# Two state-space heads: another start for B's first rows, early products of zeros, another order of the whole work

## The chip, the cores and the metric

The kernel runs on one core of one Trainium2 chip. A core has TensorE (PE; PEld is its loading of weights), VectorE (DVE), ScalarE (ACT), GpSimd (POOL) and SyncE (SP, which here only issues DMAs), an on-chip memory SBUF of 128 partitions, and PSUM, eight banks of 128 x 512 float32 values in which products are summed up. TensorE writes to PSUM alone, and VectorE or ScalarE has to copy the result out (an eviction). The metric is the device time of one execution in microseconds (us); less is better.

## The reference

Two independent heads over a sequence of 2048 steps, 640 channels each; the outputs stand beside each other, 1280 columns in bfloat16.

```
A:  dt = exp(log_dt);  Lam_bar = exp(dt * Lam);  B_bar = ((Lam_bar - 1) / Lam)[:, None] * B     (complex, 640 states)
    h[t] = Lam_bar * h[t-1] + B_bar x[t]
    y[t] = 2 Re(C h[t]) + x[t] * Dskip
B:  k_shift = causal convolution of k with 4 taps per channel
    kv = k_shift * v
    y  = causal convolution of kv with ssm_k (2048 taps per channel, by FFT of length 4096) + kv * ssm_D
    out = q * y
```

## The kernel before

**Head A** cuts the 2048 steps into 128 blocks of 16 and computes the recurrence as a tree. x is loaded transposed by eight transposing DMAs (`ld_x0` to `ld_x7`, L524, two of the 16 positions each). B is loaded in three parts: the first 128 rows as they lie, real and imaginary part (`ld_Braw`, L487), and turned by ten TensorE transposes (`turn_B`, L501) whose result one copy evicts (`ev_B`, L506); the other 512 rows by transposing DMAs (`ld_B1`, `ld_B2`, L491). The upsweep (`up2`, `up1`, `up0`) is products of B with x (L556) and, from `up1` on, of 2x2 rotation blocks RR with the results below (L577). Its first ten steps are called `up21_*` (they need x6 and x7) and `up20_*` (x4 and x5), each 20 products and one eviction (L573). A short recurrence over the blocks (`coarse`, a matter of VectorE with a scan, L656) and the downsweep (`dn`, products L681 and an addition `ad`: on VectorE L699, or on ScalarE as a plain copy L697, in which case TensorE first adds the old value by a product with the identity, L679) follow; then 16 projections by C (`project`, 20 products each, L716, eviction L718, store L722).

**Head B** computes the long convolution as a two-step Fourier transform by matrix products: a first step `s1` (L832, eviction `e1`, L837) with the table F1, a second step `s2` (L850, eviction L863) with the table W, the product of the two spectra (`product`, L874 to L881, on VectorE or POOL), and the way back in `r2` (L895, L900) and `r1` (L916, L928), then stores (L940). This is done in two halves of 320 channels. The convolution with four taps (`conv`, L797 and L798, taps by L197 on VectorE or L198 on ScalarE) comes before, channel block by channel block; its results are written to HBM and read back in another layout (`plane`, `relay`).

**Parameters.** `params` loads Lambda and log_dt by three small DMAs (`ld_par`, L348), turns them by one product (`t_par`, L356), evicts them (L358) and works out rotations from them with many small instructions on VectorE, ScalarE and POOL. `setup` makes the identity I3 and the tables F1, W and IDF with iotas and sines.

**Warm steps.** `warm` multiplies the identity with itself, four products of 512 columns (L516). Nobody reads the result. There are two of them; one stands first in TensorE's list, the other last.

**What sets the order.** All of this is 759 operations with ids in the order in which `build` adds them. The string `ORDER` lists them as id, engine letter (A ScalarE, V VectorE, G POOL, T TensorE, S SyncE) and PSUM bank. `emit` issues them in this order, each engine in its own part of it, and puts in the semaphores that the data need. So the place of an operation in the list decides what it is queued behind, and its letter which engine does it. On SP's queue the order of before begins `ld_B1 ld_x6 ld_x7 ld_B2 ld_B2 ld_B1 ld_x5 ld_x4 ld_k0 ld_sk`; on ScalarE's it begins `ld_Braw ld_par ld_par ld_Braw ld_par dt ev_B`; on TensorE's `warm1 t_par turn_B up21_0 up21_8 up21_4 up21_6`.

Of the kernel before, what the change touches and what calls it, by code (L numbers as in the profile page):

```python
# [9 lines left out]
ALU = mybir.AluOpType  # L10
# [23 lines left out]
class Program:  # L34


    def __init__(self, nc, arena, psum):
        self.nc, self.arena, self.psum = nc, arena, psum
        self.ops, self.groups, self.engine_of = [], [], {}
        self.ncol = arena.shape[1]  # L40

# [177 lines left out]
def setup(c):  # L219
# [47 lines left out]
    for b, off in ((0, 6144.0), (1, 8192.0)):  # L267
# [6 lines left out]
        out=F1.rearrange("p (k s) -> p k s", s=4), in0=bc(s1.rearrange("p (k o) -> p k o", o=1), [128, 64, 4]),  # L274
        in1=bc(me4.rearrange("p (o s) -> p o s", o=1), [128, 64, 4]), op=ALU.mult), outs=[F1], ins=[s1, me4])
# [62 lines left out]
def params(c):  # L338
# [4 lines left out]
    pr = v("YS", 0, 128)  # L343
# [121 lines left out]
class PartA:  # L465
# [14 lines left out]
    def load_B(self, k):  # L480
# [12 lines left out]
        if k == 0:  # L493
            g = P.group(2)
            idn, out = c.I3[:, 0:128], c.v("BT", 0, 1280)

            def mm(e, B):
                Bb = B.bitcast(bf16)
                for r in range(2):
                    for d in range(5):  # L500
                        e.transpose(out=Bb[:, 1024 * r + 128 * d:1024 * r + 128 * d + 128], in_=raw[:, 640 * r + 128 * d:640 * r + 128 * d + 128],  # L501
                                    identity=idn)
            P.add("turn_B", {PPE: .58}, mm, ins=[raw, idn], group=g, nmm=10)

            def ev(e, B):
                c.CP[e](out=out.rearrange("p (r x) -> p r x", r=2), in_=B.bitcast(bf16).rearrange("p (r x) -> p r x", r=2)[:, :, 0:640])  # L506
            P.add("ev_B", {PDVE: .82, PACT: 1.23}, ev, outs=[out], group=g)

    def warm(self, k):

        c, P = self.c, self.c.P
        g = P.group(1)

        def mm(e, B):
            for _ in range(4):
                e.matmul(B[:, 0:512], lhsT=c.I3[:, 0:128], rhs=bc(c.I3[:, 0:1], [128, 512]), start=True, stop=True)  # L516
        P.add(f"warm{k}", {PPE: .864}, mm, ins=[c.I3], group=g, nmm=4)
# [207 lines left out]
class PartB:  # L725
# [91 lines left out]
    def s1(self, what, hf, u):  # L817
# [11 lines left out]
        def mm(e, B):  # L829
            for i in range(8):  # L830
                for b in range(2):
                    e.matmul(B[64 * b:64 * b + 64, 128 * i:128 * i + 128], lhsT=lh[i], rhs=F[:, b, :], start=True, stop=True,  # L832
                             tile_position=(0, 64 * b))
        P.add(f"s1{what}{hf}_{u}", {PPE: .45}, mm, ins=lh + [c.F1], group=g, nmm=16)
# [3 lines left out]
            out=out, in_=B.rearrange("p (n k l s) -> p k s l n", n=8, l=2, s=2)), outs=[out], group=g)  # L838
# [108 lines left out]
def build(c):  # L947

    setup(c)
    params(c)  # L950
    a, b = PartA(c), PartB(c)
    c.a, c.b = a, b
    b.load_small()
    a.warm(0)
    a.warm(1)
# [75 lines left out]
def plain_order(P):  # L1031
# [125 lines left out]
```

## Time and profile before

| | us |
|---|---|
| median of 3 runs | 204.18 (204.13 to 205.32) |
| profiled execution | 205.59 |
| its span, first to last instruction | 203.8 |
| busy: PE / PEld | 181.6 / 121.0 |
| busy: DVE / ACT / POOL | 166.1 / 138.9 / 80.0 |

The busy times are sums over the whole span; TensorE is at 89%, VectorE at 81%, ScalarE at 68%, POOL at 39%. The DMA engines moved 30.12 MB in 107544 packets, nearly all of them under 512 bytes. An engine's share of the span is an average over stages with different limits, so the stretches of 10 us, further down, tell more than this table. In the profile a line number says which line of the program an instruction stems from; "x20" is a count; what stands behind "<-" in square brackets is what ended the wait ahead of the instruction.

### The profile page before, as it was taken

How to read it: one execution, taken by the hardware profiler on the slowest of the kernel's cores; microseconds unless marked ns; L12 is line 12 of the kernel's file. 1: busy time of each engine (PE TensorE's matmuls, PEld its weight loads, DVE VectorE, ACT ScalarE, POOL GpSimd, SP SyncE). 2: the span in 40 equal slices, each digit the busy share in tenths (PEclk: the TensorE clock that was granted, in tenths of full speed). 3: DMA queues.
4: the chain of work that ended last, by engine and by line, in shares of the span. 5: the costliest groups of instructions: out<-in, count | busy, mean ns of one | idle time of the engine just before them, and what ended most of it. 6: DMA issues, size and time to landing. Idle time of an engine off the chain costs nothing.

```text
span 203.8 us, 6975 instructions
## 1 busy us (share of the span) xinstructions
PE 181.6 (89%) x3075; PEld 121.0 (59%) x3079; DVE 166.1 (81%) x225; ACT 138.9 (68%) x167; POOL 80.0 (39%) x64
## 2 busy tenths in 40 slices
PE   3279999999999987767798899999999999999894
PEld 0135444446666744556677666666576877787672
DVE  2194999964999499988999989899999999876931
ACT  2059975476983759999988879989877993291000
POOL 8238970039400900000023294694860506325211
DMA  6999999996998999859969963940524783374785
GB/s 121 176 191 195 133 165 200 127 192 125 182 166 229 309 131 125 181 102 168 118 169 182 119 99 100 197 67 5 120 76 94 155 208 96 107 170 122 166 181 142
DMA packets 107544, 30.12 MB, mean 148 GB/s; under 512 B 102394, under 2 KB 106874, under 8 KB 107514
## 3 DMA queue, kind: packets, MB, share of 16 engines
q1 hardware_dynamic: 107136, 29.34, 80.2%
q10 hardware_dynamic: 378, 0.34, 1.0%
q8 instruction: 24, 0.39, 1.0%
q14 instruction: 6, 0.05, 0.1%
HBM read 10.99 MB, written 7.86 MB: 93 GB/s over the span
## 4 chain that ended last, share of the span: by engine, by line
PE 68%; ACT 16%; DVE 8%; DMA 3%; issue 3%; ACTq 1%; DVEq 0%
PE acc L556 22%; PE acc L716 21%; ACT arena L863 9%; PE acc L850 5%; ACT arena L837 5%; PE acc L895 5%; PE acc L832 4%; PE acc L681 4%; PE acc L577 3%; DMA arena<-in_A_Lambda_re_dram 3%; PE acc L916 2%; DVE arena L928 1%; DVE arena L837 1%; DVE arena L550 1%; DVE arena L718 1%
## 5 line engine op out<-in xcount | busy, mean ns | idle before, releaser
L556 PE MATMUL acc<-arena 128*64 128x512 bf16 x400 | 48.6, 397 | 1.3 <-ACT arena L506 1.3
L716 PE MATMUL acc<-arena 128*128 128x320 bf16 x320 | 46.1, 299 | 1.1 <-issue 0.9
L863 ACT CAST arena<-acc 128x960 bf16<-128x960 f32 (+1 forms) x41 | 36.0, 915 | 7.4 <-PE acc L850 6.4
L716 PEld LDWEIGHTS <-arena 128*128 128x128 bf16 x320 | 30.2, 98 | 14.3 <-issue 1.4
L556 PEld LDWEIGHTS <-arena 128*64 128x64 bf16 x400 | 22.4, 111 | 24.5 <-issue 1.8
L837 ACT CAST arena<-acc 128x1024 bf16<-128x1024 f32 x31 | 30.0, 1035 | 2.8 <-PE acc L832 2.4
L850 PE MATMUL acc<-arena 128*64 128x160 bf16 x512 | 23.2, 236 | 4.4 <-ACT arena L863 3.3
L832 PE MATMUL acc<-arena 128*64 128x128 bf16 x640 | 22.7, 221 | 2.8 <-ACT arena L837 1.4
L850 PEld LDWEIGHTS <-arena 128*64 128x64 bf16 x512 | 17.8, 109 | 11.7 <-ACT arena L863 6.2
L832 PEld LDWEIGHTS <-arena 128*64 128x64 bf16 x640 | 19.1, 110 | 7.7 <-ACT arena L837 2.6
L900 ACT CAST arena<-acc 128x1024 bf16<-128x1024 f32 x16 | 15.7, 1022 | 7.5 <-PE acc L895 7.5
L797 DVE TENSOR_TENSOR arena<-arena 128x2048 bf16<-128x2048 bf16 x15 | 19.9, 1327 | 0.3
L718 DVE TENSOR_TENSOR arena<-acc,arena 128x640 bf16<-128x640 f32 x16 | 13.1, 822 | 8.6 <-PE acc L716 8.3
L877 POOL TENSOR_TENSOR arena<-arena 128x1280 bf16<-128x1280 bf16 x5 | 13.2, 2640 | 16.8 <-DVE arena L874 9.2
L699 DVE TENSOR_TENSOR arena<-acc,arena 128x1024 bf16<-128x1024 f32 x15 | 17.8, 1217 | 1.0 <-PE acc L681 1.0
L881 POOL TENSOR_TENSOR arena<-arena 128x1280 bf16<-128x1280 bf16 x5 | 13.3, 2653 | 8.3 <-DVE arena L877 8.0
L708 POOL TENSOR_TENSOR arena<-arena 128x640 bf16<-128x640 bf16 x7 | 9.7, 1398 | 17.3 <-DMA arena<-in_A_x_dram 17.3
L197 DVE TENSOR_SCALAR arena<-arena 128x2048 bf16<-128x2048 bf16 (+1 forms) x19 | 15.0, 810 | 0.3
L766 POOL TENSOR_TENSOR arena<-arena 128x80 bf16<-128x80 bf16 x2 | 1.8, 878 | 31.8 <-DVE arena L874 31.8
L198 ACT ACTIVATE arena<-arena 128x1024 bf16<-128x1024 bf16 (+3 forms) x14 | 13.8, 1013 | 0.2
L329 POOL TENSOR_TENSOR arena<-arena 128x1024 int32<-128x1024 int32 x4 | 7.5, 1896 | 14.9 <-DVE arena L420 14.9
L681 PE MATMUL acc<-arena 128*128 128x512 bf16 (+2 forms) x50 | 12.1, 328 | 0.4 <-ACT arena L863 0.4
(138 smaller groups left out, 266.7 us busy)
## 6 DMA issues: line engine op xcount, KB each, us to landing
out_dram<-arena SPq DMA_DIRECT2D x32, 160.0 KB, 3.2
arena<-in_B_ssm_k_dram SPq DMA_DIRECT2D x8, 320.0 KB, 6.7
kv_rows<-arena SPq DMA_DIRECT2D x5, 512.0 KB, 3.2
arena<-kv_rows SPq DMA_DIRECT2D x8, 320.0 KB, 6.5
arena<-in_A_x_dram SPq DMA_DIRECT2D x16, 160.0 KB, 2.4
arena<-in_B_q_dram SPq DMA_DIRECT2D x8, 320.0 KB, 5.8
arena<-in_A_B_im_dram ACTq DMA_DIRECT2D x1, 160.0 KB, 2.6
arena<-in_A_B_re_dram ACTq DMA_DIRECT2D x1, 160.0 KB
```

Source lines behind the costliest of these rows:

```text
L197: vm = lambda e: lambda out, in_, by: e.tensor_scalar_mul(out=out, in0=in_, scalar1=by)
L556: e.matmul(o[64 * r:64 * r + 64], lhsT=self.BT[j][:, r, d, :], rhs=self.XP[:, d, 2 * q:2 * q + 2], start=(d == 0), stop=(d == 4), skip_gro ...
L681: e.matmul(B[:, o:o + 128 * k], lhsT=c.RR[:, n, j, :], rhs=A[:, j, q:q + k, 0:128], start=not by_pe, stop=True, skip_group_check=True)
L699: e.tensor_tensor(out=o, in0=b, in1=o, op=ALU.add)
L716: e.matmul(B[:, 512 * b:512 * b + 320], lhsT=lh[j], rhs=self.CT[:, j, 320 * b:320 * b + 320], start=(j == 0), stop=(j == 9))
L718: P.add(f"ev_C{i}", {PDVE: dve(640)}, lambda e, B: e.tensor_tensor(out=ys.rearrange("p (b n) -> p b n", b=2), in0=B.rearrange("p (b n) -> ...
L797: P.add(f"ca{d}_{j}", tt, lambda e: e.tensor_tensor(out=t1, in0=t1, in1=t2, op=ALU.add), outs=[t1], ins=[t1, t2])
L832: e.matmul(B[64 * b:64 * b + 64, 128 * i:128 * i + 128], lhsT=lh[i], rhs=F[:, b, :], start=True, stop=True, tile_position=(0, 64 * b))
L837: P.add(f"e1{what}{hf}_{u}", {PACT: act(1024), PDVE: dve(1024)}, lambda e, B: c.CP[e](out=out, in_=B.rearrange("p (n k l s) -> p k s l n", ...
L850: e.matmul(B[64 * s:64 * s + 64, 512 * b + 160 * i:512 * b + 160 * i + 160], lhsT=c.W[:, k, 64 * b:64 * b + 64], rhs=self.AS[hf][:, k, 160 ...
L863: c.CP[e](out=out, in_=b.rearrange("p r (k j n) -> p r k j n", k=n, j=4) if nj > 1 else b.rearrange("p r (k x) -> p r k x", k=n))
L900: P.add(f"er2{hf}_{u}", {PACT: act(1024), PDVE: dve(1024)}, lambda e, B: c.CP[e](out=out, in_=B.rearrange("p (s n b) -> p b s n", s=2, n=4 ...
```

## The change

It has five parts.

1. **B's first rows.** `turn_B` and `ev_B` become two operations each, one for the real and one for the imaginary half: five transposes into one PSUM bank and one copy of 640 columns. In the new order both raw loads stand first on ScalarE's queue, and the three `ld_par` are on SP's.
2. **Products of zeros.** Six warm steps of two products each in place of two of four; they multiply a block of zeros in YS, which POOL clears (`wz`), and not the identity. The parameters' landing place moves from YS 0 to YS 1280 to make room. All six stand in the first part of TensorE's list, and none at its end.
3. **F1** is stored with its columns in another order (position within 32 innermost), and the first step's eviction reads PSUM accordingly.
4. **Narrow first steps.** An `s1` step whose letter in the order is a lower-case `t` computes its products on half the rows and half the columns; one with `T` computes them as before. The new list holds capital letters only.
5. **A new order**, with other engines for some 80 operations and other PSUM banks. The ids shift, since the warm steps are now added first: an id of before plus seven is the same operation, apart from the warm steps and the turning of B. By name, SP's list now begins `ld_sk ld_par ld_par ld_par ld_x6 ld_x7 ld_B1 ld_B1 ld_x5 ld_x4 ld_k0 ld_B2 ld_B2 ld_x2 ld_x3`; ScalarE's `ld_Braw ld_Braw dt rn rn rn ev_B1 rn ev_B0 ev_up21_0` (`ev_B0` the real half, `ev_B1` the imaginary, `rn` a short exponential); TensorE's `turn_B0 warm2 t_par warm4 warm1 warm5 turn_B1 warm0 warm3 up21_0 up21_4 up21_2 up20_0 up20_2 up20_4 up21_6 up20_8 up20_6`. The coarse recurrence's first product (`cs_v0`) stands ahead of the scaling of C (`gC`) in the new list and behind most of it in the old one. Of the additions of the downsweep `ad2_5`, `ad1_2`, `ad1_0` and `ad0_0` go from VectorE to ScalarE, `ad3_5` and `ad0_9` come back. Eight half products of the spectra go from POOL to VectorE and one the other way; the last two steps of the convolution's fourth channel block (`ca3_0`, `cx3`) go from VectorE to POOL.

```diff
@@ setup
     P.add("f1", {V: .42}, lambda e: e.tensor_tensor(
-        out=F1.rearrange("p (k s) -> p k s", s=4), in0=bc(s1.rearrange("p (k o) -> p k o", o=1), [128, 64, 4]),
-        in1=bc(me4.rearrange("p (o s) -> p o s", o=1), [128, 64, 4]), op=ALU.mult), outs=[F1], ins=[s1, me4])
+        out=F1.rearrange("p (b s k) -> p b s k", b=2, s=4), in0=bc(s1.rearrange("p (b o k) -> p b o k", b=2, o=1), [128, 2, 4, 32]),
+        in1=bc(me4.rearrange("p (o s x) -> p o s x", o=1, x=1), [128, 2, 4, 32]), op=ALU.mult), outs=[F1], ins=[s1, me4])
@@ params
-    pr = v("YS", 0, 128)
+    pr = v("YS", 1280, 128)
@@ load_B
         if k == 0:
-            g = P.group(2)
-            idn, out = c.I3[:, 0:128], c.v("BT", 0, 1280)
-
-            def mm(e, B):
-                Bb = B.bitcast(bf16)
-                for r in range(2):
+            idn = c.I3[:, 0:128]
+            for r in range(2):
+                g, out, part = P.group(1), c.v("BT", 640 * r, 640), raw[:, 640 * r:640 * r + 640]
+
+                def mm(e, B, part=part):
                     for d in range(5):
-                        e.transpose(out=Bb[:, 1024 * r + 128 * d:1024 * r + 128 * d + 128], in_=raw[:, 640 * r + 128 * d:640 * r + 128 * d + 128],
-                                    identity=idn)
-            P.add("turn_B", {PPE: .58}, mm, ins=[raw, idn], group=g, nmm=10)
...
+                        e.transpose(out=B.bitcast(bf16)[:, 128 * d:128 * d + 128], in_=part[:, 128 * d:128 * d + 128], identity=idn)
+                P.add("turn_B", {PPE: .29}, mm, ins=[part, idn], group=g, nmm=5)
+                P.add("ev_B", {PDVE: .5, PACT: .7}, lambda e, B, out=out: c.CP[e](out=out, in_=B.bitcast(bf16)[:, 0:640]), outs=[out], group=g)
@@ warm
+        z = c.v("YS", 0, 130)
+        if k == 0:
+            P.add("wz", {PDVE: .1, PPOOL: .25}, lambda e: e.memset(z, 0.0), outs=[z])
+
         def mm(e, B):
-            for _ in range(4):
-                e.matmul(B[:, 0:512], lhsT=c.I3[:, 0:128], rhs=bc(c.I3[:, 0:1], [128, 512]), start=True, stop=True)
-        P.add(f"warm{k}", {PPE: .864}, mm, ins=[c.I3], group=g, nmm=4)
+            for _ in range(2):
+                e.matmul(B[:, 0:512], lhsT=z[:, 0:128], rhs=bc(z[:, 128:129], [128, 512]), start=True, stop=True)
+        P.add(f"warm{k}", {PPE: .432}, mm, ins=[z], group=g, nmm=2)
@@ s1
-                    e.matmul(B[64 * b:64 * b + 64, 128 * i:128 * i + 128], lhsT=lh[i], rhs=F[:, b, :], start=True, stop=True,
-                             tile_position=(0, 64 * b))
+                    if o.id not in P.narrow:
+                        e.matmul(B[64 * b:64 * b + 64, 128 * i:128 * i + 128], lhsT=lh[i], rhs=F[:, b, :], start=True, stop=True,
+                                 tile_position=(0, 64 * b))
+                        continue
+                    for l in range(2):
+                        ps = slice(64 * l, 64 * l + 64)
+                        e.matmul(B[64 * b:64 * b + 64, 512 * l + 64 * i:512 * l + 64 * i + 64], lhsT=lh[i][ps], rhs=F[ps, b, 64 * l:64 * l + 64],
+                                 start=True, stop=True, tile_position=(64 * l, 64 * b))
...
-            out=out, in_=B.rearrange("p (n k l s) -> p k s l n", n=8, l=2, s=2)), outs=[out], group=g)
+            out=out, in_=(B.rearrange("p (l n s k) -> p k s l n", l=2, n=8, s=2) if o.id in P.narrow
+                          else B.rearrange("p (n l s k) -> p k s l n", n=8, l=2, s=2))), outs=[out], group=g)
@@ build
+    a, b = PartA(c), PartB(c)
+    c.a, c.b = a, b
+    for k in range(6):
+        a.warm(k)
     setup(c)
     params(c)
...
-    a.warm(0)
-    a.warm(1)
@@ ORDER
-    "110G0 85V0 49V0 124A0 51A0 461G0 19G0 116G0 43G0 86V0 128S0 52A0 6G0 7V0 11V0 13V0 20V0 15G0 0G0 1G0 2V0 122T2 3V0 123A0 50A0 "
...
+    "128A0 92V0 38G0 91V0 122S0 56V0 58S0 59S0 129A0 8G0 26G0 127V0 7G0 9V0 117G0 130T2 0G0 3T4 41G0 50G0 13G0 15V0 19V0 34V0 57S0 "
+    "12V0 61T1 62V1 5T4 2T6 95V0 35V0 144S0 94V0 21V0 33V0 126G0 63A0 64V0 32V0 65V0 68A0 71V0 72V0 73V0 66A0 6T5 16V0 74V0 75V0 "
...
@@ the entry
-    order = [(int(x[:-2]), x[-2], int(x[-1])) for x in ORDER.split()] if ORDER else plain_order(c.P)
+    order = [(int(x[:-2]), x[-2].upper(), int(x[-1])) for x in ORDER.split()] if ORDER else plain_order(c.P)
+    c.P.narrow = {int(x[:-2]) for x in ORDER.split() if x[-2] == "t"}
```

More of the change, by code (lines that the diff above doesn't have):

```diff
@@ L40, in __init__ @@
         self.ncol = arena.shape[1]
+        self.narrow = set()
     def group(self, nb):
@@ L831, in mm @@
                 for b in range(2):
-                    e.matmul(B[64 * b:64 * b + 64, 128 * i:128 * i + 128], lhsT=lh[i], rhs=F[:, b, :], start=True, stop=True,
-                             tile_position=(0, 64 * b))
-        P.add(f"s1{what}{hf}_{u}", {PPE: .45}, mm, ins=lh + [c.F1], group=g, nmm=16)
+                    if o.id not in P.narrow:
[6 more added lines that the diff above has]
+                                 start=True, stop=True, tile_position=(64 * l, 64 * b))
+        o = P.add(f"s1{what}{hf}_{u}", {PPE: .45}, mm, ins=lh + [c.F1], group=g, nmm=16)
         gh, n0 = u // 5, 8 * (u % 5)
```

5 lines of the change are left out of this document (removed), and 69 rows, old and new, of the table ORDER.

## The prediction

> **What bounds the kernel now.** I read the chain that ended last first, then the stretches of 10 us, then the instructions of the first 20 us. The chain, at its start and at its end:
>
> ```profile
> 2.79 6.42 DMA arena<-in_A_Lambda_re_dram
> ...
> 9.34 0.18 PE acc L356
> 9.52 1.17 PE acc L501 x10
> ...
> 10.71 1.24 ACT arena L506
> ...
> 11.99 26.62 PE acc L556 x205
> ...
> 200.20 0.84 DVE arena L718
> ...
> 201.31 0.82 PE acc L516 x3
> ```
>
> The first product that counts (L556) starts at 11.99 us. Ahead of it lie a parameter load that took 6.42 us, the parameter product, ten transposes and their copy. From then on the chain is nearly all TensorE. The stretches (start:end, busy time of PE, PEld, DVE, ACT, POOL with counts, clock, DMA share, GB/s) say where that holds:
>
> ```profile
> 0.00:10.00 10.00, 2.55 (x11) 1.12 (x12) 1.52 (x12) 1.50 (x2) 5.75 (x19) 1.00 0.93 146
> 10.00:20.00 10.00, 8.69 (x65) 4.18 (x64) 7.15 (x32) 6.94 (x11) 5.60 (x5) 1.00 1.07 196
> 20.00:30.00 10.00, 10.00 (x90) 4.88 (x88) 9.15 (x7) 9.07 (x13) 8.86 (x10) 1.00 1.15 151
> ...
> 80.00:90.00 10.00, 6.46 (x152) 5.04 (x154) 9.32 (x13) 9.71 (x11) 0.00 (x0) 1.00 0.81 161
> 90.00:100.00 10.00, 7.30 (x194) 6.12 (x188) 9.27 (x11) 9.59 (x12) 0.00 (x0) 1.00 1.13 126
> ```
>
> Three regimes: until 12 us TensorE waits for data; from 12 us the upsweep is TensorE's own work; from 80 to 100 us TensorE is idle for 3.54 + 2.70 us because ScalarE (9.71, 9.59) and VectorE (9.32, 9.27) cannot empty PSUM faster, while POOL does nothing.  So a microsecond saved before 12 us is a microsecond of lead, and the question is whether the middle gives it back.
>
> **The parts of the change.** The profiled execution took 205.59 us, a span of 203.8 and 1.8 around it, 1.4 above the median of 204.18. My terms are differences worked out in its own time; I set them against the median.
>
> *The start.* The early instructions:
>
> ```profile
> 1.16 0.72 ACTq L348 DMA_DIRECT2D arena<-in_A_Lambda_im_dram  x1
> 1.91 0.29 ACTq L348 DMA_DIRECT2D arena<-in_A_log_dt_dram  x1
> 2.24 0.52 ACTq L487 DMA_DIRECT2D arena<-in_A_B_re_dram  x1
> 2.79 0.84 ACTq L348 DMA_DIRECT2D arena<-in_A_Lambda_re_dram  x1
> 3.42 1.89 PE L516 MATMUL acc<-arena 128*128 128x512 bf16 x4 [3.42 <-DVE arena L230]
> 9.56 0.19 DVE L358 COPY arena<-acc 128x30 f32<-128x30 f32 x1 [5.96 <-PE acc L356]
> 12.42 0.18 PEld L556 LDWEIGHTS <-arena 128*64 128x64 bf16 x2 [0.25 <-issue]
> 14.98 1.11 PEld L556 LDWEIGHTS <-arena 128*64 128x64 bf16 x10 [0.25 <-issue]
> 17.93 0.58 SPq L747 DMA_DIRECT2D arena<-in_B_shift_k_dram  x1
> ```
>
> The new order puts both raw loads of B's first rows on ScalarE's queue with nothing before them; the three parameter loads go to SP's queue behind the shift taps and ahead of every transposing load. The first raw load of before landed 2.6 us after its issue:
>
> ```profile
> L487 ACTq DMA_DIRECT2D arena<-in_A_B_im_dram x1: 381/381/381, 0.7 to 0.7; - x1
> ...
> DMA to landing us min/median/max: 2.6/2.6/2.6
> ```
>
> So the real part lands at about 3.4 us and its five transposes (half of 1.17 us) end near 4.0. One warm step of two products at 1.89/4 = 0.47 us each takes TensorE to 4.9. SP issues the taps (0.58) and three parameter loads (0.72 + 0.29 + 0.84 at ScalarE's prices, 0.87 if each took the shortest) by 2.2 to 3.2 us, then 2.6 us to landing: the parameter product at about 5.5, bounds 4.8 and, with the 6.42 us of the chain, 9. Three warm steps (6 x 0.47 = 2.8 us) and five transposes follow: 8.9. ScalarE copies the imaginary half, a short exponential, then the real half. The nearest row for half a copy:
>
> ```profile
> L550 ACT CAST arena<-acc 128x640 bf16<-128x640 f32 x7 | 4.7, 692 | 3.9 <-PE acc L577 2.1 <-PE acc L546 1.7
> ```
>
> Two at 0.69 and the exponential (0.2) end at about 10.5; the last four warm products (1.9 us) end about then, too. With 0.2 for waits the upsweep starts at 10.7 instead of 11.99: **-1.3 us** (bounds -2.5, if the warm products speed up early, and 0, with the late parameters). The twelve zero products replace eight, and as ordered they are ahead of the upsweep, so they cost nothing only as long as the copies end later.
>
> *The pace of the first products.* At 12.42 us weights are loaded in pairs every 0.43 us; from 14.98 on ten take 1.11 us, 0.11 each. In the 2.99 us between 11.99 and 14.98 there are 16 loads, which at the later pace take 1.78: 1.2 us lost to a slow clock (the clock column says 1.00 here, so the pace is the better witness). In before TensorE worked from 3.42 to 5.31, stood still until 9.34 and had 1.35 us of work before the upsweep. In the new order it works from 3.4 with one short wait. I take the whole loss back: **-1.2 us** (bounds -1.2 and 0). The Trainium skill (TensorE: Matmul & The Clock Gate, Part 1) has the full clock follow a busy window of about 3.4 us of a counter that runs on its own, and Part 4 adds that transposes don't count as busy in the same way; by that, a start broken up by transposes and waits may still be cold, which is a rival below.
>
> *What the upsweep then waits for.* Its first step needs the transposing loads x6 and x7, the next two B's second part, the fourth x5 and x4. Two landings of before bracket eight such loads:
>
> ```profile
> L491 SPq DMA_TRANSPOSE arena<-in_A_B_im_dram x1: 1372/1372/1372, 0.7 to 0.7; - x1
> ...
> DMA to landing us min/median/max: 5.5/5.5/5.5
> ...
> L524 SPq DMA_TRANSPOSE arena<-in_A_x_dram x1: 1614/1614/1614, 14.4 to 14.4; - x1
> ...
> DMA to landing us min/median/max: 4.1/4.1/4.1
> ```
>
> First at 6.2, eighth at 18.5: one per 1.76 us, with the DMA share at 0.93 to 1.07. In the new order the first is issued at about 3.0 and lands near 7.5, x7 at 9.3, B's second part at 12.8, x4 at 16.3. Wanted: 10.7, 13.0 (one step of 20 products at 0.113 is 2.26 us) and 17.5. Close, but in time: **+0.2 us** (bounds 0 and 1.0).
>
> *Work moved between engines.* Read by name, the new order moves some 80 instructions. Where the addition of a downsweep step is on ScalarE, TensorE must first add the old value by a product with the identity (L679). Four steps go to ScalarE (six products of 512 columns, four of 256) and two come back (two of 512, five of 128):
>
> ```profile
> 136.17 0.22 PE acc L679
> ...
> 103.15 0.11 PE acc L679
> ...
> L699 DVE TENSOR_TENSOR arena<-acc,arena 128x1024 bf16<-128x1024 f32 x15 | 17.8, 1217 | 1.0 <-PE acc L681 1.0
> L877 POOL TENSOR_TENSOR arena<-arena 128x1280 bf16<-128x1280 bf16 x5 | 13.2, 2640 | 16.8 <-DVE arena L874 9.2 <-PE acc L850 7.6
> L877 DVE TENSOR_TENSOR arena<-arena 128x1280 bf16<-128x1280 bf16 x11 | 9.7, 907 | 0.2
> L797 DVE TENSOR_TENSOR arena<-arena 128x2048 bf16<-128x2048 bf16 x15 | 19.9, 1327 | 0.3
> ```
>
> Six of 0.22 and four of 0.11, less two of 0.22 and five of 0.06 to 0.11, is 0.8 to 1.0 us of TensorE. A third may fall where it idles: **+0.6 us** (bounds 0 and 1.0). VectorE takes over seven spectral half products net, which took POOL 2.64 us each and take it 0.9 (6.3 in all), and gives away two long convolution steps (1.3 each at L797's mean), two of the additions net (1.2 each) and, net, some tap products, scalings and evictions; I take the sum as even, with ScalarE loaded more than before. What counts is the place: between 80 and 100 us POOL, idle now, takes the two convolution steps, 2.6 of VectorE's 18.6 us. If the two full engines shared that relief, TensorE's wait would shrink by 1.3; for ScalarE's added work I take off 0.5: **-0.8 us** (bounds -3 and +3, about half of the 6.2 us idle there either way, since no row shows the middle in another order).
>
> *The rest.* The list of the new order holds no lower-case letter, so the set `narrow` is empty and every first step keeps its wide products. What changes for them is the order of F1's columns and the strides by which the eviction reads PSUM: taken as nothing, bounded by 40 evictions times 28 ns (1035 for L837 against 1007 ns for the plain read of L573):
>
> ```profile
> L837 ACT CAST arena<-acc 128x1024 bf16<-128x1024 f32 x31 | 30.0, 1035 | 2.8 <-PE acc L832 2.4
> L573 ACT CAST arena<-acc 128x1024 bf16<-128x1024 f32 x9 | 9.0, 1007 | 3.8 <-PE acc L556 3.8
> L722 SPq DMA_DIRECT2D out_dram<-arena x1: 332/332/332, 201.1 to 201.1; - x1
> ```
>
> The dead warm step at 201.31 goes, but the last store is issued at 201.1 and lands after 2 to 3 us, so the end stays: 0.
>
> Sum: -1.3 - 1.2 + 0.2 + 0.6 - 0.8 = -2.5; 204.2 - 2.5 = **201.7 us**.
>
> **The rivals.**
>
> *The clock is still slow at 10.7 us.* Against it: over 5 us of products ahead. For it: the four early products of before, 1.89 us, never sped up. The 1.2 us stay: 202.9.
>
> *The lead is given back at 80 us.* There the two evicting engines decide, and ScalarE has more to do than before. Only the relief of POOL's two steps would remain: 204.2 - 0.5 = 203.7.
>
> *POOL holds VectorE* (slower). A long POOL instruction stops VectorE's when that reads two operands from SBUF or runs fast:
>
> ```profile
> 13.39 2.33 POOL L449 TENSOR_TENSOR arena<-arena 128x1280 int32<-128x1280 int32 x1 [6.87 <-DVE arena L378]
> ...
> L268 DVE TENSOR_SCALAR arena<-arena x2: 241/1306/2370, 3.0 to 13.4; 128x32 int32<-128x32 int32 x2
> ```
>
> One of L268's two 32-column instructions took 0.24 us; the other, started with POOL's at 13.4, took 2.37. The Trainium skill (GPSIMD Engine Reference, Specifications) names the same two cases for the shared SBUF interface; the row agrees. The two convolution steps on POOL come to 2.64 x 2048/1280 = 4.2 us each, an estimate from L877. The coarse chain's last step of the second half stands just behind the first of them in VectorE's list; if it is held for 4.2 us while both evicting engines are the bound, and ScalarE's added work eats the rest of the lead (another 0.8 lost instead of won), the time is 201.7 + 0.8 + 4.2 = 206.7. It decides from about 2.5 us of hold.
>
> *The middle does better.* The coarse chain is started ahead of the C scaling, so that downsweep products can fill the 6.2 us of idle TensorE. Half of it filled: 201.7 - 3.1 = 198.6.
>
> **How the numbers follow.** Forecast 201.7 (its own range 200.2 to 203): 0.42. Middle better, 198.6: 0.12. Slow clock, 202.9: 0.10. Lead given back, 203.7: 0.13. POOL holds VectorE, 206.7: 0.23. A measurement of this kernel tells about 1% from no change (202.1 to 206.2). Faster: the better middle and most of the forecast, 0.54; same: the rest of it, slow clock and given back, with a little of the held case, 0.24; slower 0.22. The range: 198.4 to 206.6 leaves out half of the held case and the far tail of the better middle.
>
> **What would show it.** The upsweep's first product at 10 to 11 us with weight loads 0.11 us apart from the start; the parameter product near 5.5; no TensorE wait for DMA between 13 and 25 us; L679 with four to six more columns' worth of products (about 0.9 us); POOL busy in 80 to 100 us and no VectorE instruction of two SBUF operands much above its median there. The prediction is wrong if TensorE's idle time from 80 to 100 us, 6.2 us now, grows by more than the 2.5 us of lead, or if the parameters land at 9 us again.

## The result, and the profile after

| | before | after |
|---|---|---|
| median of 15 runs, us | 205.22 (203.99 to 205.95) | 202.33 (201.56 to 204.01) |
| ratio of the times | | 0.9877 (0.9851 to 0.9903) |
| profiled execution / its span, us | 205.59 / 203.8 | 204.01 / 202.2 |
| busy PE / DVE / ACT / POOL, us | 181.6 / 166.1 / 138.9 / 80.0 | 184.9 / 164.5 / 141.2 / 77.1 |

The change makes the kernel 1.23% faster (0.97 to 1.49%), 2.9 us between the medians; forecast were 2.5 us, 1.2%. The time itself lies 0.6 us above the forecast 201.7, since that was reckoned from before's first three runs (204.18), and its median of 15 is 205.22. The two profiled executions are only 1.6 us apart, because that of after is one of its slowest; why will be seen below. Behind `load_B` the new program's lines are shifted: L573 and L577 are still the upsweep's eviction and rotations, `s1` is L833, its eviction L843, `s2` L857, its eviction L870.

The chain that ended last, of after (start us, length us, what):

```profile
2.49 1.45 SPq L524
...
7.62 4.68 DMA arena<-in_A_B_im_dram
...
23.55 1.28 ACT L369
...
25.07 1.28 ACT L395
...
198.32 0.82 DVE arena L718
```

The head of the chain is now SP's queue with the transposing loads, up to the landing of B's second part (7.62 + 4.68 = 12.30 us); then it is TensorE, broken at 23.5 us by two loads of ScalarE's function tables. The last eviction starts at 198.32 and not at 200.20 us.

The instructions of the first part of after (start us, busy us, engine, line, what, count; in brackets the wait ahead):

```profile
3.27 0.69 PE L501 MATMUL acc<-arena 128*128 128x128 bf16 x5 [3.27 <-DVE arena L242]
4.61 0.23 PE L357 MATMUL acc<-arena 128*128 128x30 bf16 x1
8.64 1.89 POOL L291 TENSOR_TENSOR arena<-arena 128x1024 int32<-128x1024 int32 x1 [0.34 <-DVE arena L247]
8.64 2.07 DVE L269 TENSOR_SCALAR arena<-arena 128x32 int32<-128x32 int32 x2
9.41 1.95 PEld L556 LDWEIGHTS <-arena 128*64 128x64 bf16 x20 [0.68 <-ACT arena L503]
12.44 14.06 PE L556 MATMUL acc<-arena 128*64 128x512 bf16 x120 [0.58 <-DMA arena<-in_A_B_im_dram]
27.59 7.00 PE L556 MATMUL acc<-arena 128*64 128x512 bf16 x60 [1.09 <-ACT arena L573]
34.43 0.60 PE L577 MATMUL acc<-arena 128*64 128x512 bf16 x4
```

The real half of B is turned at 3.27, the parameter product stands at 4.61, the first product that counts at 9.41 us. Its 20 weight loads (1.95 us busy) stand in one unbroken row, and the 20 products take 2.45 us: the pace is the full one. TensorE then waits 0.58 us for B's second part and at 26.5 us 1.09 for ScalarE. The first rotations (L577) start at 34.43 us. In before they start four microseconds later, with 20 products more done by then:

```profile
38.45 0.60 PE L577 MATMUL acc<-arena 128*64 128x512 bf16 x4
```

The stretches of after (start:end, busy time of PE, PEld, DVE, ACT, POOL with counts, clock, DMA share, GB/s):

```profile
0.00:10.00 10.00, 6.71 (x29) 3.05 (x31) 5.93 (x37) 3.29 (x8) 6.44 (x20) 1.00 0.74 143
...
80.00:90.00 10.00, 8.40 (x180) 6.53 (x182) 8.09 (x11) 9.81 (x13) 4.51 (x2) 1.00 0.79 131
90.00:100.00 10.00, 8.77 (x197) 6.82 (x196) 8.79 (x10) 9.62 (x12) 4.84 (x2) 1.00 1.36 157
```

Between 80 and 100 us TensorE is now idle for 1.60 + 1.23 = 2.83 us, 3.4 less than before. That is not a gain of the whole: other stretches that were nearly full now have gaps (TensorE is busy for 9.39 and not 9.91 us between 60 and 70, for 9.54 and not 10.00 between 130 and 140). Over the whole span TensorE's idle time falls from 203.8 - 181.6 = 22.2 to 202.2 - 184.9 = 17.3 us, and the first 10 us alone account for 7.45 - 3.29 = 4.2 of these 4.9. But products that nobody reads count as busy there (5.4 us of them in after, 1.9 in before), so this idle time doesn't measure the gain.

### The profile page after: what moved, and what is told of

It is laid out like the page before. It is cut to its first block, busy times and chain, and to the rows that moved or that the text cites. A ratio compares the mean times of both kernels' runs of the same rounds, so it can differ in the third digit from the quotient of the medians.

```text
span 202.2 us, 6998 instructions
## 1 busy us (share of the span) xinstructions
PE 184.9 (91%) x3086; PEld 123.6 (61%) x3086; DVE 164.5 (81%) x224; ACT 141.2 (70%) x168; POOL 77.1 (38%) x64
## 4 chain that ended last, share of the span: by engine, by line
PE 70%; ACT 15%; DVE 4%; SPq 3%; issue 3%; DMA 2%; DVEq 0%; ACTq 0%
PE acc L716 22%; PE acc L556 20%; ACT arena L870 8%; PE acc L902 6%; PE acc L857 5%; PE acc L833 5%; PE acc L577 4%; ACT arena L843 3%; PE acc L923 3%; PE acc L681 2%; DMA arena<-in_A_B_im_dram 2%; SPq L524 2%; PE acc L546 1%; DVE arena L718 1%; DVE arena L843 1%
## 5 line engine op out<-in xcount | busy, mean ns | idle before, releaser
L870 ACT CAST arena<-acc 128x960 bf16<-128x960 f32 (+1 forms) x41 | 36.3, 918 | 4.7 <-PE acc L857 2.9
L556 PEld LDWEIGHTS <-arena 128*64 128x64 bf16 x400 | 23.6, 108 | 23.5 <-ACT arena L573 2.1
L843 ACT CAST arena<-acc 128x1024 bf16<-128x1024 f32 x29 | 27.9, 1035 | 4.6 <-PE acc L833 4.5
L708 POOL TENSOR_TENSOR arena<-arena 128x640 bf16<-128x640 bf16 x10 | 13.8, 1396 | 38.9 <-DMA arena<-in_A_x_dram 38.9
L857 PE MATMUL acc<-arena 128*64 128x160 bf16 x512 | 23.5, 236 | 4.0 <-ACT arena L870 1.6
L857 PEld LDWEIGHTS <-arena 128*64 128x64 bf16 x512 | 17.9, 109 | 12.1 <-ACT arena L870 4.7
L833 PE MATMUL acc<-arena 128*64 128x128 bf16 x640 | 22.0, 221 | 1.4 <-ACT arena L843 1.0
L907 ACT CAST arena<-acc 128x1024 bf16<-128x1024 f32 x17 | 16.8, 1030 | 8.1 <-PE acc L902 8.0
L833 PEld LDWEIGHTS <-arena 128*64 128x64 bf16 x640 | 19.0, 110 | 4.6 <-ACT arena L843 1.7
L199 ACT ACTIVATE arena<-arena 128x1024 bf16<-128x1024 bf16 (+2 forms) x13 | 17.6, 1365 | 2.3 <-DMA arena<-in_B_k_dram 1.7
L718 DVE TENSOR_TENSOR arena<-acc,arena 128x640 bf16<-128x640 f32 x16 | 13.2, 822 | 7.0 <-PE acc L716 3.6
L797 DVE TENSOR_TENSOR arena<-arena 128x2048 bf16<-128x2048 bf16 x14 | 17.1, 1223 | 1.5 <-ACT arena L199 1.3
L437 POOL TENSOR_TENSOR arena<-arena 128x1280 bf16<-128x1280 bf16 x2 | 5.7, 2850 | 31.8 <-DVE arena L198 24.4
L843 DVE CAST arena<-acc 128x1024 bf16<-128x1024 f32 x11 | 13.3, 1221 | 3.7 <-PE acc L833 3.5
L699 DVE TENSOR_TENSOR arena<-acc,arena 128x1024 bf16<-128x1024 f32 (+1 forms) x13 | 15.1, 1185 | 1.4 <-PE acc L681 0.7
L884 POOL TENSOR_TENSOR arena<-arena 128x1280 bf16<-128x1280 bf16 x3 | 7.8, 2611 | 17.4 <-DVE arena L881 13.5
L935 DVE TENSOR_TENSOR arena<-acc,arena 128x960 bf16<-128x960 f32 (+1 forms) x12 | 11.9, 1038 | 1.8 <-PE acc L923 1.8
L198 DVE TENSOR_SCALAR arena<-arena 128x2048 bf16<-128x2048 bf16 (+1 forms) x20 | 12.3, 630 | 0.5 <-DMA arena<-in_B_k_dram 0.2
```

Source lines behind the costliest of these rows:

```text
L199: self.SM = {nc.scalar: lambda out, in_, by: nc.scalar.mul(out, in_, by), nc.vector: vm(nc.vector), nc.gpsimd: vm(nc.gpsimd)}
L556: e.matmul(o[64 * r:64 * r + 64], lhsT=self.BT[j][:, r, d, :], rhs=self.XP[:, d, 2 * q:2 * q + 2], start=(d == 0), stop=(d == 4), skip_gro ...
L699: e.tensor_tensor(out=o, in0=b, in1=o, op=ALU.add)
L718: P.add(f"ev_C{i}", {PDVE: dve(640)}, lambda e, B: e.tensor_tensor(out=ys.rearrange("p (b n) -> p b n", b=2), in0=B.rearrange("p (b n) -> ...
L797: P.add(f"ca{d}_{j}", tt, lambda e: e.tensor_tensor(out=t1, in0=t1, in1=t2, op=ALU.add), outs=[t1], ins=[t1, t2])
L843: P.add(f"e1{what}{hf}_{u}", {PACT: act(1024), PDVE: dve(1024)}, lambda e, B: c.CP[e](out=out, in_=(B.rearrange("p (l n s k) -> p k s l n" ...
```

## The experiments

Two theories stood at the start. **A:** the gain is the lead won in the first 12 us, and the rest of the order is neutral. **B:** the gain comes from the middle (additions, POOL's convolution steps), and the start only makes it visible. The kernels differ from after or before in the order, in engine letters, or in the few lines shown.

### Each half alone

`new_start_old_rest`: the new list up to the first upsweep step, then the operations that are left in the old order, with the old engines and banks; SP's first loads of B are those that the old steps ask for first.

```diff
@@ ORDER
-"... 473G0 37V0 134S0 23V0 83G0 18V0 135S0 27V0 42G0 47G0 143S0 80G0 181T3 182A3 185T5 28V0 ..."
+"... 473G0 37V0 137S0 23V0 83G0 18V0 136S0 27V0 42G0 47G0 80G0 468G0 93V0 135S0 20V0 10V0 ..."
```

> The changed program with its new list only up to the first upsweep step; behind it the operations stand in the order, on the engines and in the banks of the kernel before (B's second and third part loaded in the sequence which the old upsweep wants). Theory A, the gain is made ahead of the upsweep and kept: upsweep from 9.4 us at 0.11 us per load, ratio to before 0.983 to 0.990. Theory B, the gain is made by the new order of the middle: ratio 0.997 or more, with TensorE idle for about 6 us or more between 78 and 98 us.

`old_start_new_rest`: the old list up to the first upsweep step, the new one behind it; four products of zeros stand at the head and four tiny ones behind them.

```diff
@@ ORDER
-"128A0 92V0 38G0 91V0 122S0 56V0 58S0 59S0 129A0 8G0 26G0 127V0 ..."
+"0G0 117G0 92V0 56V0 129A0 58A0 468G0 26G0 123G0 50G0 93V0 135S0 ..."
```

> The other way round: the old list up to the first upsweep step (parameters on ScalarE's queue, eight transposing loads as before, four early products of zeros and four tiny ones), the new list behind it. Theory A: upsweep from about 12 us, its first products 0.2 us apart, ratio 0.995 to 1.003. Theory B: ratio 0.985 to 0.992, TensorE idle for about 3 us between 82 and 102 us.

Measured: 1.001 (0.9979 to 1.0042) and 0.9989 (0.9952 to 1.0025). Neither half shows a gain, though a gain of 0.2 or 0.5% would lie within these intervals. TensorE's instructions, first of the new start with the old rest, then of the old start with the new rest (its lines are one higher):

```profile
9.18 2.45 PE L556 MATMUL acc<-arena 128*64 128x512 bf16 x20 [0.60 <-ACT arena L503]
12.18 2.50 PE L556 MATMUL acc<-arena 128*64 128x512 bf16 x20 [0.55 <-DMA arena<-in_A_B_re_dram]
16.00 2.48 PE L556 MATMUL acc<-arena 128*64 128x512 bf16 x20 [1.32 <-DMA arena<-in_A_B_re_dram]
19.00 18.37 PE L556 MATMUL acc<-arena 128*64 128x512 bf16 x160 [0.51 <-ACT arena L573]
37.20 0.59 PE L577 MATMUL acc<-arena 128*64 128x512 bf16 x4
```

```profile
10.26 25.09 PE L557 MATMUL acc<-arena 128*64 128x512 bf16 x200 [0.84 <-ACT arena L503]
35.18 0.60 PE L578 MATMUL acc<-arena 128*64 128x512 bf16 x4
```

The old sequence of upsweep steps asks for more of B's rows before x5 and x4. Started early, it waits for loads (0.55, 1.32 us), and of the lead of 2.8 us at 9.18 (against 11.99) 1.2 are left at the rotations (37.20 against 38.45). The new sequence behind the old start reaches them at 35.18; with the step that it hasn't done by then added (the account below) that is 37.44, also 1.0 before the profile of before and 0.2 before another profile with its list (37.64, in `before_adds_moved`). Its own start was 1.7 us earlier than before's, at 10.26: the parameter product stood at 8.16 and not at 9.34, and B's rows are copied in two parts. Both theories fall as put: the start is worth something only to a sequence of loads and steps that can use it, and the new rest, which holds that sequence and the middle, shows no gain by itself.

### The zeros

`no_warm`: each warm step is one product of 64 columns.

```diff
@@ warm
-            for _ in range(2):
-                e.matmul(B[:, 0:512], lhsT=z[:, 0:128], rhs=bc(z[:, 128:129], [128, 512]), start=True, stop=True)
+            e.matmul(B[:, 0:64], lhsT=z[:, 0:128], rhs=bc(z[:, 128:129], [128, 64]), start=True, stop=True)
```

> The changed kernel with each of the six warm steps cut to one product of 64 columns. If the products of zeros bring the clock up: the upsweep starts between 8.6 and 9.4 us, but its first 14 or so loads are 0.2 us apart, and the time is 0.4 to 1.2 us above that of the changed kernel (ratio 0.990 to 0.994). If they do nothing, or only delay the turning of the imaginary half: pace and start as in the changed kernel or better, ratio 0.983 to 0.988.

Measured: 0.9908 (0.9877 to 0.9939). TensorE's instructions in the first 14 us (lines one lower):

```profile
8.81 0.22 PEld L555 LDWEIGHTS <-arena 128*64 128x64 bf16 x4 [2.98 <-ACT arena L503]
9.25 0.20 PEld L555 LDWEIGHTS <-arena 128*64 128x64 bf16 x2 [0.22 <-issue]
...
12.66 1.27 PEld L555 LDWEIGHTS <-arena 128*64 128x64 bf16 x12 [0.23 <-issue]
```

Without zeros the loads stand in pairs 0.43 us apart, as in before, until 12.66 us, 3.85 us after TensorE's work began; with them the pace is full from the first. So products of zeros count as activity for the clock. They are worth little here (0.9908 against 0.9877, with overlapping intervals): without them the imaginary half is turned sooner and the first product stands at 8.84 us, and with a slow pace TensorE reaches B's second part late enough not to wait for it. The rotations start at 33.24 us; in four profiles with the zeros and the same list up to there (`F1_as_before`, `conv_on_V`, `adds_as_before`, `all_narrow`) the first product stands at 9.06 to 9.83 and the rotations start at 32.25 to 32.93, only 0.3 to 1.0 us sooner. The Trainium skill (TensorE: Matmul & The Clock Gate, Part 1) lets the full clock follow a busy window of about 3.4 us; the 3.85 us agree.

### The wait at 26.5 us

In after, ScalarE's list has the last short exponential (L369) behind a long tap (L199) and an eviction, and just ahead of a sine (L395), so two table loads of 1.28 us fall where an eviction is due. The tap of the profile shown:

```profile
20.63 2.00 ACT L199 ACTIVATE arena<-arena 128x2048 bf16<-128x2048 bf16 x1 [1.70 <-DMA arena<-in_B_k_dram]
```

`exp_early` moves the exponential behind `ev_B0`; `exp_early_tap_late` also moves a long tap (`cm0_2`, L199, 2 us) behind the upsweep's eviction.

```diff
@@ ORDER, exp_early
-"... 70A0 131A2 4T5 ... 187T5 69A0 87G0 88A0 ..."
+"... 70A0 131A2 69A0 4T5 ... 187T5 87G0 88A0 ..."
@@ ORDER, exp_early_tap_late, further
-"... 82G0 341A0 79G0 ... 140S0 176A0 54V0 ..."
+"... 82G0 79G0 ... 140S0 176A0 341A0 54V0 ..."
```

> The changed kernel with one token moved: the last of the five short exponentials stands behind the copy of B's real half instead of between two sines at 23.5 us, so ScalarE loads its tables twice less (2 x 1.28 us) just when TensorE waits for its evictions. Theory A with the waits at 24 and 26 us as what gave the lead back: TensorE's wait of 1.6 us ahead of its loads at 27.59 goes, 1.0 to 1.6 us less than the changed kernel, ratio 0.980 to 0.983. If the middle sets the time: ratio 0.986 to 0.989, as the changed kernel.

> The run with the early exponential, and besides one tap product of 2 us on ScalarE (it waits for k's load) moved behind the evictions that stand next in its list. If the evictions behind that wait are what is left of the upsweep's stall: 0.3 to 0.8 us below the run with the early exponential, ratio 0.981 to 0.984. If nothing waits there any more: the same, 0.984 to 0.987.

> The changed kernel once more, beside the three that follow: ratio to before 0.985 to 0.990. Its profile tells how much of the waits of the first one (0.58 us for B's second part at 12 us, 1.6 us for ScalarE's eviction ahead of 27.6 us) comes back: if they belong to the order, the first product of the next level (L577) starts at 34 us or later; if the first profile was an unlucky one for the loads, at 33 us or earlier.

> The run with the early exponential once more, to settle whether it beats the changed kernel: it does if its ratio is again 0.986 or less (two runs of the changed kernel gave 0.988 and 0.990); the first level of the upsweep ends at 33 us or earlier in its profile.

Measured: `exp_early` 0.9856 (0.981 to 0.9902) and again 0.9884 (0.9843 to 0.9925); after once more 0.9901 (0.9862 to 0.9941); `exp_early_tap_late` 1.0052 (1.0015 to 1.0088). The rotations of after's second profile start at 33.94 us, between the 33 and the 34 that were to decide. TensorE in `exp_early`, then in `exp_early_tap_late`:

```profile
12.41 20.62 PE L556 MATMUL acc<-arena 128*64 128x512 bf16 x180 [0.52 <-DMA arena<-in_A_B_im_dram]
32.85 0.62 PE L577 MATMUL acc<-arena 128*64 128x512 bf16 x4
```

```profile
33.05 3.98 PE L556 MATMUL acc<-arena 128*64 128x512 bf16 x20 [2.61 <-POOL arena L437]
36.85 0.61 PE L577 MATMUL acc<-arena 128*64 128x512 bf16 x4
```

The wait goes, and the rotations start 1.6 us sooner than in the profiled execution of after. But the medians (202.12 and 202.20 against 202.33 and 202.51) differ by 0.1 to 0.4 us with overlapping intervals, and `F1_as_before`, which has after's own list, shows 200 products without any wait behind the first, as do `adds_as_before` and `all_narrow` with the same list up to there:

```profile
9.80 23.04 PE L556 MATMUL acc<-arena 128*64 128x512 bf16 x200 [0.55 <-ACT arena L503]
32.66 0.62 PE L577 MATMUL acc<-arena 128*64 128x512 bf16 x4
```

So the wait at 26.5 us is a matter of the two profiled executions of after (204.01 and 204.02 us), which are 1.5 to 1.7 above their medians, and, as far as the other profiles tell, not of its usual one. What separates them is the load of k that ScalarE's first long tap (L199) waits for. The tap starts at 20.63 and 20.18 us in the two profiles of after, behind waits of 1.70 and 1.11 us for that load, and at 18.34 to 19.27, behind waits of at most 0.35, in the five other profiles with this list; the tables and the evictions follow at the same distance (the first table load at 23.55 against 21.57 in `F1_as_before`). In `exp_early` and its repetition the tap starts at 18.87 without a wait, so they don't show what the moved exponential is worth when k comes late. Why it came late is open.

The late tap shows the other side. VectorE needs it for the convolution, stands still for 5.40 us, and so delays the rotations' factors on POOL (L437). TensorE waits 2.61 us for these, and in this wait its clock falls: the column says 0.97 between 32 and 33 us and 0.50 from 33 to 36, and the next 20 products take 3.98 us, where `exp_early` needs 2.45. The 4.0 us at L577 against `exp_early` become 3.4 us of time.

### What the middle is worth

`conv_on_V` gives POOL's two convolution steps back to VectorE; `adds_as_before` undoes the six moved additions; `before_adds_moved` makes them alone in the old kernel; `F1_as_before` has F1's old columns and eviction strides.

```diff
@@ ORDER, conv_on_V
-"408G0 ... 409G0"
+"408V0 ... 409V0"
@@ ORDER, adds_as_before
-"299V0 ... 305A4 ... 311A0 ... 309A6 ... 319A6 ... 337V2"
+"299A0 ... 305V4 ... 311V0 ... 309V6 ... 319V6 ... 337A2"
@@ ORDER of before, before_adds_moved
-"292A4 ... 298V2 ... 304V4 ... 302V0 ... 312V0 ... 330A2"
+"292V4 ... 298A2 ... 304A4 ... 302A0 ... 312A0 ... 330V2"
```

> The changed kernel with the two convolution steps of the fourth channel block back on VectorE, the list otherwise the same. If POOL relieves two full engines, as the prediction's term of -0.8 us has it: 0.5 to 1.3 us above the changed kernel, ratio 0.990 to 0.994. If POOL holds VectorE up: below it, ratio 0.984 or less. If neither decides the middle: 0.986 to 0.989.

> The changed kernel with the six moved additions of the downsweep back on the engines they had before, so that TensorE is spared 0.8 to 1.0 us of products with the identity, ScalarE about 2.5 us, and VectorE has about 2.8 us more. If TensorE sets the pace there: 0.5 to 0.9 us below the changed kernel, ratio 0.983 to 0.986. If VectorE does: above it by 1 us or more, ratio 0.992 or more.

> The kernel before with only the six additions moved as in the changed one (four to ScalarE, two to VectorE), the list otherwise untouched. If moving them is good in itself, since VectorE is the bound where they stand: ratio 0.980 to 0.992. If it fits the new list alone: 0.997 or more, 0.8 to 1.0 us of TensorE added with nothing in return.

> The changed kernel with F1's columns and the first step's eviction as before. By the prediction's term of nothing: ratio 0.985 to 0.992, evictions of the first step within 30 ns of 1035. If the strides of the eviction matter: 1 us above, ratio 0.993 or more, evictions of L842 or thereabouts slower than in the changed kernel.

Measured, in this order: 0.9917 (0.9886 to 0.9947), 1.0127 (1.0083 to 1.017), 1.0219 (1.0173 to 1.0264), 0.9897 (0.9854 to 0.994). The groups of after that matter (mean ns is the second figure behind the bar):

```profile
L843 ACT CAST arena<-acc 128x1024 bf16<-128x1024 f32 x29 | 27.9, 1035 | 4.6 <-PE acc L833 4.5
...
L797 POOL TENSOR_TENSOR arena<-arena 128x2048 bf16<-128x2048 bf16 x1 | 4.2, 4240 | 17.1 <-DVE arena L198 17.1
...
L679 PE MATMUL acc<-arena 128*128 128x256 bf16 x10 | 2.4, 276 | 0.5 <-ACT arena L843 0.3
L679 PE MATMUL acc<-arena 128*128 128x512 bf16 x6 | 2.3, 384 | 0.4 <-ACT arena L870 0.4
```

POOL's two steps take 4.24 and 4.08 us, as estimated, and hold nobody: taking them away doesn't make the kernel faster, and its median (202.71) is, if anything, a little worse. In after the coarse chain's last step (L662, two operands in SBUF) started at 85.24 us, 0.17 ahead of POOL's first, and took its usual 0.49; until POOL was done at 93.8 VectorE only emptied PSUM. So the case in which a hold was feared, POOL first, didn't arise. The eviction with the new strides takes 1035 ns, that with the old ones 1034.

The additions are the surprise. VectorE's instructions in `adds_as_before`, then the same stretch of `after_again`:

```profile
105.46 0.82 DVE L888 TENSOR_TENSOR arena<-arena 128x1280 bf16<-128x1280 bf16 x1
106.19 2.35 DVE L699 TENSOR_TENSOR arena<-acc,arena 128x1024 bf16<-128x1024 f32 x2
...
109.14 0.82 DVE L718 TENSOR_TENSOR arena<-acc,arena 128x640 bf16<-128x640 f32 x1
```

```profile
105.33 0.82 DVE L888 TENSOR_TENSOR arena<-arena 128x1280 bf16<-128x1280 bf16 x1
...
106.76 0.82 DVE L718 TENSOR_TENSOR arena<-acc,arena 128x640 bf16<-128x640 f32 x1
```

Back on VectorE, two additions stand ahead of the first projection's eviction, 2.4 us in a stretch in which VectorE is full, and everything behind starts that much later. Another 1.8 us had gone before that: the rotations of this run were 1.7 us earlier than in `after_again` (32.25 against 33.94), but at 105.4 us it is 0.1 behind. The stretch in between shows TensorE idle for 2.15 us and a granted clock of 0.83; of `after_again` the same stretch, and then 56 products of the second step in each of the two:

```profile
90.00:100.00 10.00, 7.85 (x154) 6.48 (x148) 8.28 (x9) 6.95 (x10) 3.21 (x3) 0.83 1.21 163
...
96.15 3.58 PE L857 MATMUL acc<-arena 128*64 128x160 bf16 x56 [0.46 <-ACT arena L870]
```

```profile
90.00:100.00 10.00, 8.77 (x185) 6.64 (x183) 8.80 (x10) 9.62 (x13) 4.90 (x3) 1.00 1.23 167
...
96.66 2.61 PE L857 MATMUL acc<-arena 128*64 128x160 bf16 x56 [0.26 <-ACT arena L870]
```

In `adds_as_before` the clock column says 0.50 from 96 to 99 us. The slow products alone cost 1.0 of the 1.8 us, and ScalarE and VectorE wait for them (1.18 and 1.05 us).

In the old kernel the same six moves the other way cost 2.2%, in another place. The stretch of `before_adds_moved`, and the same of before:

```profile
120.00:130.00 10.00, 8.52 (x140) 5.81 (x139) 6.19 (x7) 9.61 (x12) 3.80 (x2) 1.00 0.69 144
```

```profile
120.00:130.00 10.00, 9.45 (x168) 6.75 (x168) 9.36 (x11) 9.53 (x11) 5.28 (x3) 1.00 0.48 119
```

ScalarE is full there in both, and with the additions added to its list VectorE has less to do in that stretch, 6.19 us and not 9.36, and TensorE falls from 9.45 to 8.52. From 120 to 150 us TensorE is idle for 2.7 us against 0.6, and the added products come on top; together that is most of the 3.5 us by which the rest of this kernel is longer (the account below). So an addition's engine has no price of its own; it has one by the list around it.

### The branch that isn't used

`all_narrow` makes all 40 first steps narrow.

```diff
@@ ORDER
-"161T0 169T6 ... 151T4 153T2 ... 163T6 ..."
+"161t0 169t6 ... 151t4 153t2 ... 163t6 ..."
```

> The changed kernel with every one of the 40 first steps in the narrow form (lower-case letters): 32 products of 64 columns on half the rows in place of 16 of 128. If the four quarters of the array run at once, a step takes TensorE 0.3 us and not 0.55, and where evictions are the bound the time stays (0.985 to 0.990); if each product costs its issue and its own weight load, a step takes 0.8 us or more and the time rises by 3 us or more (ratio 1.002 or more).

Measured: 1.0263 (1.0206 to 1.0321). Its six executions show a mean granted clock of 0.95 to 0.99; the profiled one, the slowest (212.58 us), has the lowest. Its products by group and the wide ones of after, and three stretches of 2 us:

```profile
L838 PE MATMUL acc<-arena 64*64 64x64 bf16 x1280 | 17.3, 203 | 10.4 <-issue 6.4 <-ACT arena L843 2.5 <-ACT arena L870 0.7
```

```profile
L833 PE MATMUL acc<-arena 128*64 128x128 bf16 x640 | 22.0, 221 | 1.4 <-ACT arena L843 1.0 <-ACT arena L597 0.2
```

```profile
90.00:92.00 2.00, 0.97 (x115) 0.88 (x104) 0.93 (x2) 0.77 (x2) 2.00 (x1) 1.00 1.33 117
92.00:94.00 2.00, 0.68 (x57) 0.48 (x48) 1.10 (x1) 2.00 (x3) 1.43 (x2) 0.83 1.05 156
...
96.00:98.00 2.00, 2.00 (x19) 1.35 (x19) 2.00 (x3) 0.61 (x1) 0.00 (x0) 0.50 1.24 228
```

TensorE is busy for less time with these products (17.3 us against 22.0 for the wide ones), but it stands idle longer ahead of them, 10.4 us against 1.4. Of these, 6.4 us, in four waits, ended with nothing that the profile shows, each in the middle of a step: of one step, 24 of its 32 products start at 92.58, the other 8 at 95.21. What ended them is open. ScalarE and VectorE in turn wait 16.9 us for the first step's products, against 8.0 in after. More than half idle from 90 to 94 us, TensorE falls to a clock of 0.50, and the work behind is done at half the pace. The longest single gap there is 2.25 us; then 28 products of the second step in `all_narrow`, and in after:

```profile
95.21 0.32 PE L838 MATMUL acc<-arena 64*64 64x64 bf16 x8 [2.25 <-issue]
...
97.28 2.08 PE L857 MATMUL acc<-arena 128*64 128x160 bf16 x28
```

```profile
95.18 1.19 PE L857 MATMUL acc<-arena 128*64 128x160 bf16 x28 [0.38 <-DVE arena L843]
```

The clock had fallen before that gap was half a microsecond old: slices of half a microsecond say 1.00, 0.83 and 0.50 from 92.5 us on, the last product ended at 92.96, and the longest gap up to there since 84 us was 1.03. Neither expectation came true as put, since the products took less time and the kernel more.

The Trainium skill (TensorE: Matmul & The Clock Gate, "HAM oscillation — how this bites in real kernels") names idle gaps of more than about 3.4 us as what brings the slow clock; here shorter ones did.

### The account

All runs together, by two instants of each profile: the first rotations (L577) and the last eviction (L718). When the rotations start, the new list has done 200 upsweep products, the old one 220, so 2.26 us (20 products) are added for the new list.

| | L577, set even | last L718 | between |
|---|---|---|---|
| before | 38.45 | 200.20 | 161.8 |
| new start, old rest | 37.20 | 199.36 | 162.2 |
| old start, new rest | 37.44 | 199.31 | 161.9 |
| after / again | 36.69 / 36.20 | 198.32 / 198.15 | 161.6 / 162.0 |
| no_warm | 35.50 | 196.99 | 161.5 |
| conv_on_V | 35.19 | 196.90 | 161.7 |
| exp_early / again | 35.11 / 35.13 | 196.04 / 196.64 | 160.9 / 161.5 |
| F1_as_before | 34.92 | 196.21 | 161.3 |
| exp_early_tap_late | 39.11 | 200.34 | 161.2 |
| adds_as_before | 34.51 | 201.01 | 166.5 |
| before_adds_moved | 37.64 | 202.91 | 165.3 |
| all_narrow | 34.99 | 207.08 | 172.1 |

With the old or the new rest, 160.9 to 162.2 us pass behind the upsweep's first level, in eleven of fourteen profiles. So the gain of the change is the instant at which that level is done, carried one for one to the end; the late tap, 4.0 us behind `exp_early` at the first instant and 3.7 to 4.3 at the last, shows the same. Three kernels stand apart, those whose middle was damaged. A kernel with the new list through this level and the old one behind it wasn't run, so that the rest of the new order is worth nothing by itself rests on the last column.

## Why the prediction was right, point by point

The path was right: the lead is made ahead of the rotations and kept, and the middle takes nothing back. Two of its terms, for the moved work and for the middle, were each wrong and held in their sum, which is luck.

- **The start (-1.3)**: right in mechanism, too small. First product at 9.41 instead of 10.7 us: the parameter product stood at 4.61, not 5.5, and the copies were done by then. In eleven profiles with the new start it is at 8.84 to 9.98 us. But before isn't fixed either: in `before_adds_moved`, with the same list at the start, it is at 10.39, because the parameters landed at 7.6 and not at 9.2. Against that the gain is 0.4 to 1.6, against the profile shown 2.0 to 3.2 us.
- **The pace (-1.2)**: right in mechanism, too large in the sum. The twenty loads took 1.95 us in one row, and `no_warm` brings the slow pace back; the rival "slow clock" falls. But only 0.3 to 1.0 us of it reach the rotations, since the zeros also hold up the first product by 0.2 to 1.0 us, and a faster TensorE may have to wait for B's second part (0.69 us in `conv_on_V`).
- **The upsweep's waits (+0.2)**: the landing of B's second part was taken as 12.8, and was 12.30 us; since the upsweep came earlier, it waited 0.58 us. The wait at 26.5 us, with the late load of k behind it, was not seen at all. In the profiled executions of after the rotations start 1.0 to 2.2 us later than in the profiles without it; in those it costs nothing.
- **The sum of the first level (-2.3)**: 38.45 - 36.69 = 1.8 us in the two profiles; for the executions of the new list without the wait at 26.5 (34.92 to 35.50) 2.1 to 3.5 us, by which execution of the old list they are set against (37.64 or 38.45). The medians lie 2.9 us apart, which is within this, so nothing is left over for the middle.
- **Work moved (+0.6)**: the products were sized right (six of 512, ten of 256 and five of 128 columns now; two, six and ten before; 0.9 us more), but the step was put wrongly. As a price of its own it has the wrong sign in the new list, where undoing the moves makes the kernel 2.3% slower than `after_again`.
- **The middle (-0.8)**: TensorE's idle time from 80 to 100 us fell by 3.4, further than assumed, and the gaps came back between 60 and 70 and behind 100 us. Together with the added products it comes to about nothing: 161.8 against 161.6 to 162.0 us. The two terms were +0.6 - 0.8 = -0.2, so their sum held, by luck: the idle time came back elsewhere, and `conv_on_V` shows no price for the relief by POOL on which the -0.8 was built.
- **POOL holds VectorE (rival, 0.23)**: the price of a step was right (4.2 us), the hold didn't come, by 0.17 us of order (L662 ahead of POOL). `conv_on_V`, without these steps, isn't faster.
- **Lead given back at 80 us, and the better middle**: both rejected by the column "between".
- **F1 and the end (0)**: right, 1035 against 1034 ns; and the unused branch would have cost, not gained.

## What to carry to other kernels

A lead at the start is worth what the next stage can take up: find the instant at which the first stage that runs at its own pace is done, and compare that instant and not the first instruction. Here the halves of a searched order couldn't be priced apart; the same six moves cost 2.3% when undone in one list and 2.2% when made in another. Before TensorE's products are made shorter or moved away, ask what the idle time that this leaves does to its clock.

## What the runs showed of the hardware

Products of zeros bring TensorE's pace up: with them 20 weight loads stood in one row, without them in pairs 0.43 us apart for 3.85 us. At the start the clock column is no witness of the pace: this stretch of before says 1.00 while its loads came in pairs 0.43 us apart.

```profile
12.00:15.00 3.00, 3.00 (x16) 1.25 (x18) 2.86 (x12) 1.43 (x3) 1.61 (x1) 1.00 1.13 203
```

Further on the column and the pace agree: at 0.50 the 28 products took 2.08 and not 1.19 us. The clock fell to 0.50 in one wait of 2.61 us (`exp_early_tap_late`), and without any gap so long where TensorE had been busy for about half of the time: 1.65 of the 3.0 us ahead of 93.0 with gaps of at most 1.03 (`all_narrow`), 1.86 of the 3.5 us ahead of 95.5 with gaps of at most 0.82 (`adds_as_before`). Which share of which stretch decides wasn't tested.

One of VectorE's two instructions of 32 columns at 8.64 us of after, started with POOL's of 1.89 us, took 1.92 us and the other 0.23. POOL's convolution steps held nothing on VectorE, which was emptying PSUM beside them; why the one and not the other wasn't tried.
